# Pooled attention with its queries in blocks of 64, 64 and 16 and its keys split into 128 and 16

## The chip, the cores and the metric

The kernel runs on one core of one Trainium2 chip. The metric is the device time of one execution in microseconds (µs). Five engines work side by side, each through its own instructions in order, and wait for each other by semaphores: TensorE (PE in the profile, with PEld for its weight loads), VectorE (DVE), ScalarE (ACT), GpSimd (POOL) and SyncE (SP), which here only issues DMAs. POOL also issues the DMAs that add to what already lies in on-chip memory.

## The reference

Two attentions are added, and the sum goes through a gated layer without nonlinearity. `q`, `k` and `v` are 8 x 8 x 576 x 64 in fp32 (batch, head, position, feature).

```python
factor = 4; Sd = S // factor                       # 144 pooled positions
q_d = q.reshape(B, H, Sd, factor, D).mean(axis=3)  # and k_d, v_d
out_d = sm_attn(q_d, k_d, v_d)                     # softmax over 144 keys
out_up = np.repeat(out_d, factor, axis=2)
mask = np.abs(pos[:, None] - pos[None, :]) < factor
out_local = softmax(where(mask, scale * q @ k.T, -1e9)) @ v
x = (out_up + out_local)  ->  (4608, 512)
a = x @ w1;  b = x @ w2
out = (a * b @ w3) @ w_out
```

Only the pooled attention, `out_d`, is touched by the change.

## The kernel before

**The order of the work.** The kernel first lists all its work as tasks (`Plan.add`): an engine, an estimated cost, the tasks it depends on, and the rings of buffers it takes. `Plan.order` then plays the list through many times, backward and forward, with different allowances, and keeps the order that a replay with random delays finds best. The program is written out in that order, and within an engine the order is fixed. So a change of one task's cost can rearrange work anywhere. A ring of `n` buffers lets a task start when the task `n` before it has let go.

**The stages.** The program folds `w3 @ w_out` on PE (`accw`, line 351), splits weights into two fp32r parts, and works through 24 units (8 batches, 3 each). A unit computes the local attention and adds the pooled one; two units make a chunk of 384 tokens for the gated layer (`moe`): 24 matmuls of 384 columns into each pair of `pab` tiles (lines 269 to 271), and 9 matmuls of 512 columns into `acc` for each of eight slices. The two `pab` banks are freed by ACT (`a<-pab`, line 912) and DVE (line 914). The units of batches 0 and 1 do the local attention on PE in groups (`se_ps`, `te_ps`, `oe_ps`), those of batches 2 to 7 on DVE and ACT (`pr`, `pv`, `xl`), with some sums as accumulating DMAs on POOL (`xl<-pv`, line 842).

**The pooled attention** (`pooled` and `quad`, lines 418 to 535) is done once per batch:
- The four positions of a pool are summed. For batches 2 to 7 `qks` and `vs` are loaded once by SP and three times added to by POOL's accumulating DMAs (lines 433 and 434). For batches 0 and 1 only `vs` is. `vs` holds the 144 keys as two halves of 72 on 72 partitions, a row of 4 KB for each.
- Heads are handled in two quads of two pairs of heads. The scores (`s_ps`, line 482) of a quad are 12 matmuls over 64 features in 64x64 tiles of PE: three blocks of queries (from 0, 48 and 80; 64 in each, so that they overlap), two pairs, two parities of the head. Each gives 144 columns.
- DVE takes the maximum (`gmx`, line 487), ACT the exponential with its sum (`pexp`, line 496; six instructions), DVE the reciprocal, and POOL (line 511), for batches 0 and 1 ACT (line 508), scales.
- PE transposes `pexp` (`t_ps`, line 521; 12 transposes per quad, to 72 partitions), and ACT copies the result into `pt` (line 528, three copies).
- PE multiplies `pt` with `vs` (`o_ps`, line 449; 32 matmuls over 72 keys in 72x32 tiles, two halves for each result), and ACT copies into `oup` (lines 457 and 459).

`pexp`, `pt`, `vs` and `qks` have one buffer each, and `s_ps`, `t_ps` and `o_ps` share three PSUM banks with the group attention.

Of the kernel before, what the change touches and what calls it, by code (L numbers as in the profile page):

```python
# [9 lines left out]
F32 = mybir.dt.float32  # L10
# [11 lines left out]
FAC = 4  # L22
SD = S // FAC
SB = SD // 16
NB = 16
# [7 lines left out]
NT = 3  # L33
THIRDS = [(0, 0), (48, 0), (80, 16)]
# [28 lines left out]
AHEAD = 4  # L63

# [15 lines left out]
class Task:  # L80
    __slots__ = ("eng", "cost", "fn", "deps", "late", "rings", "after")

    def __init__(self, eng, cost, fn, deps, late, rings, after):
        self.eng, self.cost, self.fn, self.deps, self.late, self.rings, self.after = eng, cost, fn, deps, late, rings, after


class Plan:

    def __init__(self):
        self.tasks = []  # L90

    def add(self, eng, cost, fn, deps=(), take=(), uses=(), late=0.0):
# [7 lines left out]
        t = Task(eng, cost, fn, [d for d in deps if d is not None], late, rings, after)  # L100
# [91 lines left out]

    def order(self):
# [19 lines left out]
        return [self.tasks[i] for i in self.best[3]]  # L213
# [26 lines left out]
def tile_attention_moe(ctx: ExitStack, tc: tile.TileContext, q, kw, vw, qk4, v4, w1, w2, w3, wout, edge, out):  # L240
# [15 lines left out]
    nc.scalar.activation(out=junk, in_=junk, func=AF.Exp)  # L256

# [63 lines left out]

    def out_weight(j):
# [7 lines left out]
    def fold():  # L330
# [3 lines left out]

        def block(m, hf):
            T, _, tx, h = words(w3[m, hf].unsqueeze(1), lambda: pools["early"].tile([128, 512], F32, name="w3", bufs=BUFS["w3"]), [R["w3"]], "early")
            xs[m, hf] = T, tx, h

        def product(m, j):
# [22 lines left out]

        def part(m, hf):
# [24 lines left out]
    def gate_weights(g):  # L388
# [6 lines left out]
        for wi, wsrc in enumerate((w1, w2)):  # L395
            for k0 in range(0, KT, parts):
                src = wsrc[min(g, 1), k0:k0 + parts, :, at:at + n].rearrange("k p n -> p k n")
                T, ld, tx, wx = words(src, lambda: pools[pool].tile([128, nw], F32, name="wx", bufs=BUFS[pool + "_wx"]), [R[pool + "_wx"]], pool, parts)
                ld.deps += before

                def high(T=T, wi=wi, k0=k0):
                    if gates[wi][g] is None:
                        both = [wpool, pools.get("wlate")][g - 1].tile([128, 2, KT, 2, n], F32R, name=["wo", "wb"][g - 1])
                        for i in range(2):
                            gates[i][g] = both[:, i]
                    T["p"] = gates[wi][g][:, k0:k0 + parts]
                    nc.scalar.copy(out=T["p"][:, :, 0], in_=T["x"].rearrange("p (k n) -> p k n", k=parts))
                th = add("ACT", act_us(nw), high, [tx] + (folded if g == 1 else []), uses=[wx])
                tl = add("DVE", dve_us(nw), lambda T=T: nc.vector.tensor_tensor(out=T["p"][:, :, 1], in0=T["x"].rearrange("p (k n) -> p k n", k=parts), in1=T["p"][:, :, 0].bitcast(F32), op=ALU.subtract), [th], uses=[wx])
                users += [th, tl]  # L410
                g_ready.setdefault((wi, g), []).extend([th, tl])
# [4 lines left out]

    def pooled(b):
# [6 lines left out]

        def first_v():
            raws[b][1] = work.tile([QB, 2, H, D], F32, name="vs", bufs=BUFS["vs"])
            nc.sync.dma_start(out=raws[b][1], in_=v4[b, 0])
        if b not in PB:
            lq, hq = add("SP", 0.5, first_qk, take=[R["qks"]], late=dma_us(128 * 4608))
        lv, hv = add("SP", 0.5, first_v, [lq], take=[R["vs"]], late=dma_us(QB * 4096))  # L430
        for f in range(1, FAC):
            if b not in PB:
                lq = add("Pool", 1.04, lambda f=f: nc.gpsimd.dma_start(out=raws[b][0], in_=qk4[b, f], accum_op=ALU.add), [lq], uses=[hq], late=dma_us(128 * 4608, True))
            lv = add("Pool", 1.04, lambda f=f: nc.gpsimd.dma_start(out=raws[b][1], in_=v4[b, f], accum_op=ALU.add), [lv], uses=[hv], late=dma_us(QB * 4096, True))
# [8 lines left out]
        def values():  # L443
            for dh in range(2):
                P["o", dh] = ps.tile([128, 2, SD], F32, tag="g", name="o_ps", bufs=BUFS["ps"])
# [631 lines left out]
```

## Time and profile before

| | |
|---|---|
| time, median of 3 runs | 783.5 µs (782.77 to 785.19) |
| the profiled execution's own time | 783.63 µs |
| its span, first to last instruction | 781.9 µs |
| granted TensorE clock, mean | 0.993 |
| busy: PE, DVE, ACT, POOL | 752.5, 613.0, 540.0, 115.8 µs |
| DMA packets | 42548, 111.92 MB |

The profile is one execution, and the difference of 1.7 µs between its time and its span lies ahead of the first instruction and behind the last. A line of the profile names the source line (L482), the engine, the operation, what is written and read by the program's tile names, the shapes and a count. Matmuls overlap, and the end of each is modelled: what a matmul costs is read from one start to the next, not from its duration.

### The profile page before, as it was taken

What the parts mean: (1) busy time and instruction counts of PE and PEld (TensorE: products, weight loads), DVE (VectorE), ACT (ScalarE), POOL (GpSimd) and SP (SyncE); (2) the same over time, 40 slices, a digit from 0 to 9 for tenths busy, and PEclk for the clock granted to TensorE, in tenths of its full rate; (3) what the DMA queues carried; (4) which work ended last, traced back from release to release, by engine and by line L of the source; (5) the groups of instructions that cost most, each with busy time, mean ns of one, the idle gap of its engine ahead of it and who ended that gap; (6) DMA issues with size and microseconds to landing.
All of it is one profiled execution on the core that took longest, in us unless ns stands there. A gap on an engine that the chain in (4) does not pass through costs nothing.

```text
span 781.9 us, 15058 instructions
## 1 busy us (share of the span) xinstructions
PE 752.5 (96%) x5320; PEld 654.8 (84%) x5320; DVE 613.0 (78%) x1049; ACT 540.0 (69%) x2120; POOL 115.8 (15%) x139
## 2 busy tenths in 40 slices
PE   4889999999999999999999999999999999999995
PEld 1445588898999899999999999998999999999994
DVE  4457966749999999989999998998998998963110
ACT  5788898647978688666787686776785787841211
POOL 1000011000221122211121222110221220110000
PEclk9999999999999999999999999999999999999998
DMA  8995779433576727856549739854469544350101
GB/s 291 305 252 182 230 190 218 81 104 103 117 181 177 149 63 202 202 99 171 127 88 224 172 80 216 169 119 135 119 134 224 122 114 120 63 100 1 41 0 41
DMA packets 42548, 111.92 MB, mean 143 GB/s; under 512 B 5080, under 2 KB 11224, under 8 KB 42472
## 3 DMA queue, kind: packets, MB, share of 16 engines
q0 software_dynamic: 12672, 38.94, 28.9%
q1 hardware_dynamic: 29800, 72.01, 28.5%
q8 instruction: 42, 0.69, 0.4%
q14 instruction: 34, 0.28, 0.1%
HBM read 80.26 MB, written 9.44 MB: 115 GB/s over the span
## 4 chain that ended last, share of the span: by engine, by line
PE 73%; issue 7%; DMA 7%; DVE 6%; ACT 5%; POOL 1%; SPq 1%; POOLq 0%; ACTq 0%; DVEq 0%
PE pab L269 14%; PE pab L270 14%; PE pab L271 14%; PE acc L269 7%; PE acc L271 7%; PE acc L270 7%; PE accw L351 3%; DMA raw<-in_w_dram 3%; PE t_ps L521 2%; DMA raw<-in_wout_dram 2%; PE o_ps L449 2%; ACT pexp L496 1%; DVE pr L767 1%; DMA xl<-pv 1%; PE s_ps L482 1%
## 5 line engine op out<-in xcount | busy, mean ns | idle before, releaser
L777 ACT ACTIVATE junk<-pr 128x64 f32<-128x64 f32 x432 | 110.8, 257 | 19.0 <-DVE pr L767 8.4
L767 DVE TENSOR_TENSOR pr<-q_t,kv 128x768 f32<-128x768 f32 x126 | 119.8, 973 | 3.6 <-DMA kv<-in_kw_dram 3.5
L826 ACT ACTIVATE pv<-kv,s_t 128x64 f32<-128x64 f32 x432 | 114.5, 342 | 10.3 <-DVE s_t L803 5.9
L269 PE MATMUL acc<-wphl,gh 128*128 128x512 f32 x288 | 115.5, 401 | 0.0
L271 PE MATMUL acc<-wphl,gl 128*128 128x512 f32 x288 | 113.8, 395 | 0.0
L270 PE MATMUL acc<-wphl,gh 128*128 128x512 f32 x288 | 113.6, 394 | 0.0
L912 ACT COPY a<-pab 128x384 f32<-128x384 f32 x96 | 45.9, 478 | 79.9 <-PE pab L271 66.5
L914 DVE TENSOR_TENSOR a<-pab,a 128x384 f32<-128x384 f32 x96 | 53.2, 554 | 53.5 <-PE pab L271 48.8
L842 POOL DMA_DIRECT2D xl<-pv x54 | 47.2, 875 | 311.4 <-DVE xl L844 249.7
L919 ACT CAST gh<-a 128x384 fp32r<-128x384 f32 x96 | 49.2, 513 | 59.4 <-PE acc L270 52.1
L780 DVE TENSOR_REDUCE s_t<-pr 128x12 f32<-128x768 f32 x90 | 84.1, 944 | 0.1
L777 ACT ACTIVATION_READ_ACCUMULATOR junk<-pr 128x1 f32 x432 | 81.1, 188 | 0.0
L351 PE MATMUL accw<-wo,w 128*128 128x512 f32 x128 | 64.4, 638 | 15.5 <-DVE w L316 12.2
L921 DVE TENSOR_TENSOR gl<-a,gh 128x384 fp32r<-128x384 f32 x96 | 53.9, 562 | 27.9 <-ACT gh L919 27.5
L834 DVE TENSOR_TENSOR pv<-kv,s_t 128x768 f32<-128x768 f32 x72 | 69.8, 979 | 0.1
L269 PE MATMUL pab<-xh,wo 128*128 128x384 f32 x192 | 66.3, 346 | 0.5 <-ACT a L912 0.5
L269 PE MATMUL pab<-xh,w2a 128*128 128x384 f32 x192 | 66.1, 344 | 0.3 <-DVE a L914 0.2
L269 PE MATMUL pab<-xh,w1a 128*128 128x384 f32 x192 | 66.2, 345 | 0.0
L269 PE MATMUL pab<-xh,wb 128*128 128x384 f32 x192 | 65.8, 343 | 0.2
L270 PE MATMUL pab<-xl,w2a 128*128 128x384 f32 x192 | 65.7, 342 | 0.0
L271 PE MATMUL pab<-xh,w2a 128*128 128x384 f32 x192 | 65.5, 341 | 0.0
L271 PEld LDWEIGHTS acc<-wphl,gl 128*128 128x128 f32 x288 | 54.1, 188 | 13.2
(109 smaller groups left out, 1718.6 us busy)
## 6 DMA issues: line engine op xcount, KB each, us to landing
xl<-pv POOLq DMA_DIRECT2D x54, 384.0 KB, 4.3
raw<-in_w_dram SPq DMA_DIRECT2D x32, 512.0 KB
qks<-in_qk_dram POOLq DMA_DIRECT2D x18, 576.0 KB, 7.4
kv<-in_kw_dram SPq DMA_DIRECT2D x18, 576.0 KB
kv<-in_vw_dram SPq DMA_DIRECT2D x18, 576.0 KB
vs<-in_v_dram POOLq DMA_DIRECT2D x24, 288.0 KB, 6.5
q_t<-in_q_dram SPq DMA_DIRECT2D x18, 384.0 KB
out_dram<-o_sb SPq DMA_DIRECT2D x24, 256.0 KB
```

The lines of the kernel that those rows point to most:

```text
L269: nc.tensor.matmul(out_ps, lhsT=lh, rhs=rh, start=first, stop=False)
L270: nc.tensor.matmul(out_ps, lhsT=lh, rhs=rl, start=False, stop=False)
L271: nc.tensor.matmul(out_ps, lhsT=ll, rhs=rh, start=False, stop=last)
L351: nc.tensor.matmul(accs[m], lhsT=T["x"][:, j % 4 * 128:j % 4 * 128 + 128], rhs=wo[0][:, j], start=j == 0, stop=j == NF - 1)
L767: (nc.gpsimd if o in share["qk_pool"] else nc.vector).tensor_tensor(out=T[o], in0=T["q"], in1=T["k"][:, o * D:o * D + nq].rearrange("p (t ...
L777: nc.scalar.activation(out=junk, in_=T[o][:, t], func=AF.Copy, accum_out=T["s"][:, t, o:o + 1])
L780: reds.append(add("DVE", dve_us(nq), lambda o=o: nc.vector.tensor_reduce(out=T["s"][:, :, o], in_=T[o], op=ALU.add, axis=AX.X), [tp], uses ...
L826: nc.scalar.mul(out=T["pv", o][:, tt], in_=T["v"][:, (tt + o) * D:(tt + o + 1) * D], mul=T["s"][:, tt, o:o + 1])
L834: nc.vector.tensor_tensor(out=T["pv", o], in0=T["v"][:, o * D:o * D + nq].rearrange("p (t d) -> p t d", d=D), in1=T["s"][:, :, o].unsqueez ...
L914: tg = add("DVE", dve_us(CT), lambda f=f: nc.vector.tensor_tensor(out=T["a", f], in0=T["p", 1, f], in1=T["a", f], op=ALU.mult), [ta, ends[ ...
L919: nc.scalar.copy(out=T["gh", f], in_=T["a", f])
L921: tl = add("DVE", dve_us(CT), lambda f=f: nc.vector.tensor_tensor(out=T["gl", f], in0=T["a", f], in1=T["gh", f].bitcast(F32), op=ALU.subtr ...
```

## The change

The 144 queries of all heads are now cut into 64, 64 and 16. The first quad has two blocks (queries 0 to 63 and 64 to 127 of its two pairs), the second these two and a third that holds the last 16 queries of all four pairs (it computes the last 32 and uses 16), in 64x32 tiles. The keys are split into 128 and 16: each score matmul becomes a wide one (128 columns) and a narrow one (16), and both parities lie side by side in a tile `pexp`, now allocated once for the whole kernel, with 16 columns of zeros between them, so that the 16 last keys of both heads are transposed together. A block has three transposes of 128x128 instead of four of 112 or 128 by 72.

`v` is loaded as `vs` (128 keys on 128 partitions) and `vl` (16 keys), each with its own DMAs in rows of 2 KB, and `vl` is copied once within on-chip memory to partitions 32 to 47, by ACT (by DVE for batches 0 and 1), for the other parity. The values become 16 matmuls over 128 keys and 16 over 16 keys in 32x32 tiles, the latter at row 0 for one parity and at row 32 for the other. `o_ps` is now one tile per parity instead of one per half of the features.

The planner gains names for groups of tasks and a list of shifts (`SHIFTS`), which is empty; after the search it now plays the best priorities through once more (`self.final`), with an allowance of 0.1 and transfers 1.1 times as long, and that order is written out.

```diff
-NT = 3
-THIRDS = [(0, 0), (48, 0), (80, 16)]
+QM = 64
+QR = SD - 2 * QM
+KM = 64
+KR = SD - 2 * KM
+PW = 128 + KR
...
-        return [self.tasks[i] for i in self.best[3]]
+        prio = list(self.best[1])
...
+        self.final = self.run(prio, 0.1, slow=1.1)
+        return [self.tasks[i] for i in self.final[3]]
...
+    soft = wpool.tile([128, 3, 2 * PW + 16], F32, name="pexp")
+    nc.vector.memset(soft[:, :, PW:PW + 16], 0.0)
...
+        def load_v(f, add=False):
+            dma = (lambda **kw: nc.gpsimd.dma_start(accum_op=ALU.add, **kw)) if add else nc.sync.dma_start
+            return [lambda: dma(out=raws[b][1], in_=v4[b, f, :KM].rearrange("p k h d -> k p (h d)")),
+                    lambda: dma(out=raws[b][2][:KR], in_=v4[b, f, KM:].rearrange("p k h d -> k p (h d)"))]
...
-            lv = add("Pool", 1.04, lambda f=f: nc.gpsimd.dma_start(out=raws[b][1], in_=v4[b, f], accum_op=ALU.add), [lv], uses=[hv], late=dma_us(QB * 4096, True))
+            lv = [add("Pool", 1.04, ld, [t], uses=[hv], late=dma_us(n * 2048, True)) for ld, t, n in zip(load_v(f, True), lv, (128, KR))]
+        if b in PB:
+            lv.append(add("DVE", dve_us(H * D, True), lambda: nc.vector.tensor_copy(out=raws[b][2][32:], in_=raws[b][2][:KR]), lv[1:], uses=[hv]))
+        else:
+            lv.append(add("ACT", act_us(H * D), lambda: nc.scalar.copy(out=raws[b][2][32:], in_=raws[b][2][:KR]), lv[1:], uses=[hv]))
...
-                    for kb in range(2):
-                        for Q in range(NQ):
-                            nc.tensor.matmul(P["o", dh][32 * Q:32 * Q + 32, par], lhsT=raws[b][1][:, kb, 2 * Q + par, dh * 32:dh * 32 + 32], rhs=P["pt"][:, Q, par, kb], start=kb == 0, stop=kb == 1)
+                    for Q in range(NQ):
+                        h = (2 * Q + par) * D + dh * 32
+                        nc.tensor.matmul(P["o", par][32 * Q:32 * Q + 32, dh], lhsT=raws[b][1][:, h:h + 32], rhs=P["pt"][:, Q, par], start=True, stop=False)
+                for par in range(2):
+                    r = 32 * par
+                    for Q in range(NQ):
+                        h = (2 * Q + par) * D + dh * 32
+                        nc.tensor.matmul(P["o", par][32 * Q:32 * Q + 32, dh], lhsT=raws[b][2][r:r + KR, h:h + 32], rhs=P["pt"][r:r + KR, Q, 2], start=False, stop=True)
...
+        nt = 2 + qd
...
-            for i, (q0, _) in enumerate(THIRDS):
-                for w in range(2):
+            for i in range(nt):
+                m, ws, q0 = (32, range(NQ), SD - 32) if i == 2 else (QM, (2 * qd, 2 * qd + 1), QM * i)
+                for w, pair in enumerate(ws):
                     for par in range(2):
-                        qk = raws[b][0][par * D:par * D + D, :, 2 * qd + w]
-                        nc.tensor.matmul(T["s"][par][w * GQ:w * GQ + GQ, i], lhsT=qk[:, 0, q0:q0 + GQ], rhs=qk[:, 1], start=True, stop=True)
+                        qk = raws[b][0][par * D:par * D + D, :, pair]
+                        ks = qk[:, 1].rearrange("p (k s) -> p k s", k=2)
+                        for of, at in ((ks[:, :, :KM], KR * par), (ks[:, :, KM:], 128 * (1 - par))):
+                            nc.tensor.matmul(T["s"][par][w * m:w * m + m, i, at:at + of.shape[1] * of.shape[2]], lhsT=qk[:, 0, q0:q0 + m], rhs=of, start=True, stop=True)
...
-                for par in range(2):
-                    for kb in range(2):
-                        nc.tensor.transpose(out=T["t"][i][:, par, kb, :n], in_=T["p"][:n, par, i, kb * QB:kb * QB + QB], identity=ident[:n, :n])
+                for x, at in enumerate((0, PW + 16 + KR, 128)):
+                    nc.tensor.transpose(out=T["t"][i][:, x], in_=T["p"][:, i, at:at + 128], identity=ident)
```

On PE, at the first scores of batch 2 (`s_ps` from `qks`, between matmuls of the gated layer), there stood before

```order
L269 MATMUL pab<-xh_1649,w2a 128x384
L270 MATMUL pab<-xl_1650,w2a 128x384
L271 MATMUL pab<-xh_1649,w2a 128x384
L482 MATMUL s_ps<-qks 64x144 x12
L269 MATMUL acc_1209<-wphl,gh 128x512
```

and there stands now

```order
L301 MATMUL pab<-xh_1681,w1a 128x384
L302 MATMUL pab<-xl_1682,w1a 128x384
L303 MATMUL pab<-xh_1681,w1a 128x384
L547 MATMUL s_ps<-qks 64x128
L547 MATMUL s_ps<-qks 64x16
```

where the last two rows follow each other eight times in all, sixteen times in the second quad. A wide and a narrow matmul of the same tile stand next to each other.

On PE, at the values of batch 2 (`o_ps`, ahead of the third group of gate weights before and of the first now), there stood before

```order
L269 MATMUL pab<-xh_2049,w2a 128x384
L270 MATMUL pab<-xl_2050,w2a 128x384
L271 MATMUL pab<-xh_2049,w2a 128x384
L449 MATMUL o_ps<-pt,vs 32x144 x32
L269 MATMUL pab<-xh_2049,wo 128x384
```

and there stands now

```order
L301 MATMUL pab<-xh_2083,w2a 128x384
L302 MATMUL pab<-xl_2084,w2a 128x384
L303 MATMUL pab<-xh_2083,w2a 128x384
L504 MATMUL o_ps<-pt,vs 32x144 x8
L509 MATMUL o_ps<-pt,vl 32x144 x8
L504 MATMUL o_ps<-pt,vs 32x144 x8
L509 MATMUL o_ps<-pt,vl 32x144 x8
```

The block keeps its number of matmuls, in four runs that change between tiles of 128x32 and 32x32.

On POOL, at the accumulations of v of batch 5 (`qks` is the load of queries and keys, `xl` a sum of the local attention), there stood before

```order
L433 DMA qks<-in_qk_dram 128x1152
L434 DMA vs<-in_v_dram 72x1024
L842 DMA xl<-pv 128x768
L434 DMA vs<-in_v_dram 72x1024 x2
L842 DMA xl<-pv 128x768
```

and there stands now

```order
L482 DMA qks<-in_qk_dram 128x1152
L467 DMA vl<-in_v_dram 16x1x512
L467 DMA vs<-in_v_dram 128x1x512
L915 DMA xl<-pv 128x768
L467 DMA vl<-in_v_dram 16x1x512
L467 DMA vs<-in_v_dram 128x1x512
L467 DMA vl<-in_v_dram 16x1x512
L467 DMA vs<-in_v_dram 128x1x512
```

Six issues stand where three stood, and the third of `vl` comes behind the second of `vs`.

More of the change, by code (lines that the diff above doesn't have):

```diff
@@ L90, in __init__, with named, run @@
         self.tasks = []
+        self.group = ""
+    def named(self, fn):
+        def run(*a):
+            old, self.group = self.group, " ".join([fn.__name__] + [str(x) for x in a if isinstance(x, int)])
+            r = fn(*a)
+            self.group = old
+            return r
+        return run
     def add(self, eng, cost, fn, deps=(), take=(), uses=(), late=0.0):
@@ L99, in add @@
             after += last[:1]
-        t = Task(eng, cost, fn, [d for d in deps if d is not None], late, rings, after)
+        t = Task(eng, cost, fn, [d for d in deps if d is not None], late, rings, after, self.group)
         for h in list(got) + list(uses):
@@ L191, in replay, with again @@
         return max(end)
+    def again(self, prio):
+        now = self.run(prio, 0.1)
+        back = self.run([-x for x in now[2]], 0.05, back=True, slow=1.1)
+        return [-x for x in back[2]]
     def order(self):
@@ L394, in gate_weights @@
         parts = 512 // n
-        for wi, wsrc in enumerate((w1, w2)):
-            for k0 in range(0, KT, parts):
[L397 to L411, printed above, removed]
@@ L827, in unit @@
                     if t0 == 0:
[L828 removed]
+                        tm, h = add("ACT", TOKENS * act_us(D, 1), mult, [norm, lv], take=[ring], uses=[hv, hs])
                     else:
```

123 lines of the change are left out of this document (84 added, 39 removed).

## The prediction

> **What bounds the kernel now.** I read the page's first part, then the windows by stage, then who waits for whom on the matrix engine (PE), then its timeline.
>
> ```profile
> PE 752.5 (96%) x5320; PEld 654.8 (84%) x5320; DVE 613.0 (78%) x1049; ACT 540.0 (69%) x2120; POOL 115.8 (15%) x139
> ```
>
> The busy share says PE, but a pipelined matmul can look busy while it waits. The windows (busy time of each engine, granted clock, DMA share, GB/s) and the waits of PE from 160 µs on settle it:
>
> ```profile
> 20.00:60.00 40.00, 35.76 (x202) 17.23 (x200) 21.04 (x47) 30.14 (x74) 2.65 (x3) 1.00 0.95 281
> 60.00:100.00 40.00, 37.43 (x455) 20.16 (x449) 33.49 (x87) 35.68 (x106) 0.00 (x0) 1.00 0.61 193
> 100.00:160.00 60.00, 58.90 (x783) 52.26 (x784) 40.65 (x101) 49.37 (x178) 7.74 (x9) 0.97 0.68 157
> ...
> 180.00:680.00 500.00, 499.04 (x3205) 458.27 (x3204) 466.38 (x715) 382.63 (x1671) 98.28 (x104) 1.00 0.61 142
> 680.00:782.00 102.00, 92.56 (x481) 85.73 (x480) 31.34 (x51) 25.70 (x63) 3.42 (x4) 0.96 0.17 39
> ```
> ```profile
> PE pab L269 <- ACT a L912: 0.5, 1, 0.5
> PE pab L269 <- DVE a L914: 0.2, 1, 0.2
> ```
>
> From 160 µs to the end PE waits 0.7 µs. The pace of its matmuls says the same (start, duration, instruction): 0.17 µs from one gate matmul to the next at 300 µs, where VectorE (DVE) is 93% busy (466.38 of 500), and again at 725 µs, where little runs beside PE.
>
> ```profile
> 300.29 0.34 PE L270 MATMUL pab<-xl,w1a 128*128 128x384 f32 x1
> 300.46 0.34 PE L271 MATMUL pab<-xh,w1a 128*128 128x384 f32 x1
> 300.73 0.97 PE L482 MATMUL s_ps<-qks 64*64 64x144 f32 x24
> 301.62 0.44 PE L269 MATMUL pab<-xh,w2a 128*128 128x384 f32 x1
> ```
> ```profile
> 724.98 0.34 PE L271 MATMUL pab<-xh,w1a 128*128 128x384 f32 x1
> 725.15 0.34 PE L269 MATMUL pab<-xh,w2a 128*128 128x384 f32 x1
> ```
>
> So PE time removed after 160 µs is taken off the end. The tile view of the values' result (copies per batch two: first and last start) says which batches lie there: 2 to 7, while 0 and 1 are done by 125 µs, where PE waits for weights:
>
> ```profile
> L459 ACT COPY oup<-o_ps x12: 377/390/402, 248.1 to 655.3; 128x288 f32<-128x288 f32 x12
> L457 ACT COPY oup<-o_ps x4: 398/400/418, 59.2 to 125.3; 128x288 f32<-128x288 f32 x4
> ```
> ```profile
> PE accw L351 <- DVE w L316: 12.2, 4, 8.3
> ```
>
> I count nothing for them.
>
> **The change on PE.** What a block costs is the distance from its first start to the next block's. Two blocks in 64x64 tiles (scores with 144 and group scores with 72 columns) and two in 72x32 tiles (values with 144 and group values with 64) give the price of a column:
>
> ```profile
> 149.22 0.64 PE L655 MATMUL se_ps<-k,qn 64*64 64x72 f32 x24
> 149.79 0.44 PE L269 MATMUL pab<-xh,wb 128*128 128x384 f32 x1
> ```
> ```profile
> 316.69 2.17 PE L449 MATMUL o_ps<-pt,vs 72*32 72x144 f32 x64
> 318.79 0.44 PE L269 MATMUL pab<-xh,wb 128*128 128x384 f32 x1
> ```
> ```profile
> 165.58 1.56 PE L697 MATMUL oe_ps<-pte,v_w 72*32 72x64 f32 x96
> 167.06 0.50 PE L269 MATMUL acc<-wphl,gh 128*128 128x512 f32 x1
> ```
>
> An fp32 matmul is two passes (x24 for 12 matmuls), and four tiles fit the array, so I count rounds of four passes. Scores: 6 rounds of 144, 864 columns, 0.89 µs; group scores: 432 columns, 0.57; so 0.74 ns a column and 0.25 fixed. Values: 16 rounds of 144, 2304 columns, 2.10; group values: 24 rounds of 64, 1536 columns, 1.48; so 0.81 ns and 0.24 fixed. Entering a tiled block costs 0.09 besides (0.27 from 300.46 to 300.73, less 0.18). Per batch before: scores 2 x 0.98 = 1.96, values 2.19.
>
> The transposes run untiled:
>
> ```profile
> 48.08 1.37 PE L521 MATMUL t_ps<-ident,pexp 112*72 112x112 f32 x12
> 49.28 1.02 PE L351 MATMUL accw<-wo,w 128*128 128x512 f32 x2
> ```
> ```profile
> 68.41 0.82 PE L626 MATMUL te_ps<-ident,se 128*72 128x128 f32 x6
> 69.06 0.60 PE L351 MATMUL accw<-wo,w 128*128 128x512 f32 x1
> ```
>
> Twelve cost 1.20, so 2.40 per batch; one with 128 columns costs 0.65/6 = 0.108.
>
> After the change:
> - **Scores.** The first quad has two blocks, each of four wide (128 keys) and four narrow (16 keys) matmuls: 576 columns and four narrow rounds. The second has a third block of eight tiles of 64x32; if eight run at once it adds 288 columns. By columns alone: 0.09 + 0.25 + 0.43 = 0.77 and 0.09 + 0.25 + 0.64 = 0.98. A narrow round costs between its 0.012 by columns and the 0.052 of a 64-column round (64 x 0.81); I add 0.02 to each of the ten, halfway, as no row is nearer. The change of tiling ahead of the third block costs between nothing and 0.34 (a fixed part and an entry); I take the entry's 0.09, the only row of such a change by itself. So 0.85 + 1.19 = 2.04: **+0.08**. Eight tiles at once is not in the trace; in both modes it shows, as many run as fit, so I take eight. Four would add 0.21.
> - **Transposes.** 6 + 9 full ones: 15 x 0.108 = 1.62, **-0.78**. Weights of 128 columns instead of 72 are loaded for each; if that set the pace, the 0.175 of a gate matmul, which loads as many, is the upper bound: 2.63, +0.23.
> - **Values.** 16 matmuls over 128 keys (8 rounds) and 16 over 16 keys in 32x32 tiles (4 rounds if eight run at once): 1728 columns, 0.09 + 0.24 + 1.40 = 1.73. They alternate, three changes of tiling inside; at 0.09 each 2.00: **-0.19**. Bounds: 1.73 with free changes; 0.47 more with four at once and 1.02 for changes at 0.34, 3.22.
>
> Per batch 2.04 + 1.62 + 2.00 = 5.66 for 6.55: **-0.89**, and -5.3 µs for six. The profiled execution took 783.63 (span 781.9 and 1.7 around it), 0.13 over the median of 783.5. **Forecast 778.3 µs.** At the lower bounds (narrow and tiling free) the batch saves 0.21 + 0.78 + 0.46 = 1.45; for all eight 11.6, 772. At the upper ones scores cost 0.93 + (0.98 + 0.24 + 0.34 + 0.21) = 2.70, and the batch loses 0.74 + 0.23 + 1.03 = 2.0: 799.6. All upper ends together need four misreadings of one sign.
>
> The narrow matmuls are where a page speaks against the change: the Trainium skill, "TensorEngine Tiling", section "Instruction Overhead", gives each matmul about 60 cycles, so that a narrow one costs as much as one with 60 columns. As an estimate by that page a narrow round is 60 x 0.74 = 0.044 instead of 0.032, 0.12 more per batch, and the sum would give 779.0; no row here has fewer than 64 columns.
>
> **The other engines.** Grouped by shape (count, busy, mean ns):
>
> ```profile
> L496 ACT ACTIVATE pexp<-s_ps,gnb 128x144 f32<-128x144 f32 x96 | 35.4, 386 | 2.4 <-DVE gnb L488 2.0
> L511 POOL TENSOR_TENSOR pexp<-pexp,grs 128x432 f32<-128x432 f32 x24 | 29.6, 1261 | 93.5 <-ACT pv L826 51.7 <-DVE grs L504 29.6 <-ACT junk L777 11.6
> L434 POOL DMA_DIRECT2D vs<-in_v_dram x24 | 22.9, 956 | 139.0 <-DMA vs<-in_v_dram 138.0 <-PE pab L271 0.9
> L929 ACT COPY o_sb<-acc 128x512 f32<-128x512 f32 x36 | 20.5, 580 | 8.5 <-DMA out_dram<-o_sb 6.8 <-PE acc L271 1.6
> L496 ACT ACTIVATION_READ_ACCUMULATOR pexp<-s_ps,gnb 128x1 f32 x96 | 20.2, 211 | 0.0
> L528 ACT COPY pt<-t_ps 72x384 f32<-72x384 f32 x48 | 20.0, 474 | 0.0
> L487 DVE TENSOR_REDUCE gmx<-s_ps 128x3 f32<-128x432 f32 x32 | 18.0, 599 | 1.9 <-PE s_ps L482 1.8
> ```
>
> ScalarE (ACT) loses two exponentials per batch (2 x 0.60) and one and a half copies (0.7), and gains the copy of vl (0.58, as the 512 wide o_sb): -1.3. DVE loses a third of two maxima (0.4), POOL a third of two products (0.8), and gains three issues (2.9). All of it lies beside PE (383, 466 and 98 of 500 busy), so it counts nothing. Without that cover ACT's -1.3 and DVE's -0.4 would still be gains. The bytes of v are the same, in twice as many rows of half the length; from 180 µs the DMA engines are 61% busy.
>
> **A wait is added:** ACT now waits for the last accumulation into vl, where before only PE waited for v. Behind it on ACT stand the copies `a<-pab` that free PE's two gate banks. It is tightest in batch 5, whose three issues and first exponential were:
>
> ```profile
> 430.86 0.89 POOL L434 DMA_DIRECT2D vs<-in_v_dram  x1
> ...
> 437.80 1.21 POOL L434 DMA_DIRECT2D vs<-in_v_dram  x1
> 444.46 0.83 POOL L434 DMA_DIRECT2D vs<-in_v_dram  x1 [5.45 <-DMA vs<-in_v_dram]
> ```
> ```profile
> 452.42 0.39 ACT L496 ACTIVATE pexp<-s_ps,gnb 128x144 f32<-128x144 f32 x1
> ```
> ```profile
> DMA to landing us min/median/max: 4.4/6.5/11.3
> ```
>
> The third vl issue stands behind the second of vs, so near 439; it lands near 445, and ACT comes to the copy just ahead of the exponentials, near 449. I cost it at nothing, with 4 µs to spare.
>
> **The rivals.**
> 1. *The gain is given back* (0.17): with PE faster, DVE ends the wait. For it: 93% busy from 180 to 680. Against it: PE waits 0.7 µs now. Then only DVE's six times 0.4 is left, 2.4: 781.2, or a little more with new waits: 782.
> 2. *The tiles stop overlapping in the scores* (0.11, slower): a narrow matmul stands between two wide ones of the same tile, four passes in a row. If PE starts the next tile only when the last of these has begun, a matmul pair costs 2 x 0.095 + 0.012 = 0.20 (128 columns at 0.74 ns); 8 and 16 pairs give 1.6 + 0.34 and 3.2 + 0.43, 5.6 for 1.96. The batch loses 3.6 - 0.97 = 2.7, six 16: 799. It decides from scores of 2.9 on (the gain gone), about two tiles at once. Against it: two passes of one tile stand in a row today, and 24 passes of 0.107 still take 0.89, four abreast. The Trainium skill, "TensorE: Matmul & The Clock Gate", Part 3, states the rule that would do it, "MATMULs are pc-monotone in start AND end — strict FIFO, no reordering"; by that rule today's 24 passes would take nearly twice their 0.89, so this trace does not agree.
> 3. *ACT waits for vl* (0.07): a landing of 11.3 instead of 6.5 is 4.8 late; less the 2.1 µs of one gate bank (12 x 0.175) 2.7 for each of two batches eats the gain: 783.7.
> 4. *The new order starts worse* (0.05, slower): instructions of the first 100 µs are rearranged, where loads take 95% of the DMA time; a few µs, 788.
> 5. *Narrow rounds and changes of tiling are nearly free* (0.10): 772 to 776.
>
> **How the numbers follow.** The forecast (776 to 781.2) has 0.50. With about 0.3% (2.35 µs) as what a measurement can tell from none: faster 0.50 + 0.10 = 0.60, same 0.17 + 0.07 = 0.24, slower 0.16. The range takes in rivals 1 and 3 and most of 5: 773 to 786.5.
>
> **What would show it.** PE's starts: first scores 0.76, second 1.10 without entry, six transposes 0.65, nine 0.97, values 1.91; PE's waits after 160 µs still under 2 µs. Wrong if scores take 1.5 and more (rival 2), if PE waits for `a` or DVE (1), if ACT idles ahead of `vl` (3), or if the first gate matmul starts later than before (4).

## The result, and the profile after

The changed kernel takes **1023.93 µs** (median of 4 runs, 1023.04 to 1028.5), the kernel before 784.35 on the same chip (782.77 to 785.62): a ratio of **1.308**, with a 95% interval of 1.305 to 1.311. The forecast of 778.3 and its range of 773 to 786.5 are both far off, and so is the sign. Below, a run's time is the median of all its executions, and ratios compare the fast ones alone: three runs have one slow execution each (2570, 1902 and 794.6 µs) that is in no ratio.

The page of the profiled execution (its own time 1024.09, its span 1022.3): busy times, DMA packets and the queue of the accumulating DMAs (packets, MB, share of 16 engines), the chain that ended last, and two groups of DMA issues with their median time to landing.

```profile
PE 796.1 (78%) x5632; PEld 684.2 (67%) x5632; DVE 603.0 (59%) x1052; ACT 529.7 (52%) x2082; POOL 146.7 (14%) x163
...
DMA packets 69174, 112.14 MB, mean 110 GB/s; under 512 B 29400, under 2 KB 35544, under 8 KB 69096
...
q0 software_dynamic: 38784, 39.13, 23.7%
...
DMA 44%; PE 40%; issue 8%; DVE 3%; POOL 2%; ACT 2%; SPq 1%; POOLq 0%; DVEq 0%; ACTq 0%
DMA vs<-in_v_dram 17%; DMA vl<-in_v_dram 13%; DMA xl<-pv 9%; PE pab L301 8%; PE pab L302 8%; PE pab L303 8%; PE acc L303 4%; PE acc L301 4%; PE acc L302 4%; DMA raw<-in_w_dram 1%; PE accw L386 1%; PE o_ps L504 1%; PE s_ps L547 1%; DMA k<-in_qk_dram 1%; DMA qks<-in_qk_dram 1%
...
xl<-pv POOLq DMA_DIRECT2D x54, 384.0 KB, 6.1
...
vs<-in_v_dram POOLq DMA_DIRECT2D x24, 256.0 KB, 15.0
```

PE is no longer what sets the end: the chain holds 44% of DMA, and three transfers stand at its head. An accumulation into `vs` lands in 15.0 µs where it took 6.5, with a ninth fewer bytes in it (256 KB for 288; the others are in `vl`). The queue moves the same 39 MB as in the kernel before, in three times the packets. The same rows on the page of before:

```profile
q0 software_dynamic: 12672, 38.94, 28.9%
...
xl<-pv POOLq DMA_DIRECT2D x54, 384.0 KB, 4.3
...
vs<-in_v_dram POOLq DMA_DIRECT2D x24, 288.0 KB, 6.5
```

Who waited for whom (µs in total, times, longest), the whole span:

```profile
POOL vs L467 <- DMA vs<-in_v_dram: 179.8, 15, 15.7
POOL vl L467 <- DMA vl<-in_v_dram: 152.8, 17, 68.4
...
PE pab L301 <- ACT a L987: 112.4, 15, 18.8
...
ACT vl L488 <- DMA vl<-in_v_dram: 67.8, 4, 25.7
...
DVE xl L917 <- DMA xl<-pv: 65.9, 8, 15.0
```

POOL's instructions around 350 µs (start, duration, and in brackets how long it stood idle before and for what) show how one late landing spreads:

```profile
349.37 0.92 POOL L467 DMA_DIRECT2D vl<-in_v_dram  x1 [10.77 <-DMA vl<-in_v_dram]
350.12 1.54 POOL L467 DMA_DIRECT2D vs<-in_v_dram  x1
350.93 1.67 POOL L915 DMA_DIRECT2D xl<-pv  x1
353.28 0.91 POOL L467 DMA_DIRECT2D vl<-in_v_dram  x1 [0.69 <-DMA vl<-in_v_dram]
364.69 1.35 POOL L467 DMA_DIRECT2D vs<-in_v_dram  x1 [10.50 <-DMA vs<-in_v_dram]
366.49 0.89 POOL L467 DMA_DIRECT2D vl<-in_v_dram  x1 [0.45 <-DMA vl<-in_v_dram]
367.28 1.02 POOL L915 DMA_DIRECT2D xl<-pv  x1
383.74 1.37 POOL L467 DMA_DIRECT2D vs<-in_v_dram  x1 [15.43 <-DMA vs<-in_v_dram]
384.57 2.62 POOL L577 TENSOR_TENSOR pexp<-pexp,grs 128x288 f32<-128x288 f32 x2
```

Each accumulation into `vs` waits for the one before it, and POOL runs its instructions in order, so two of them hold up POOL from 350 to 384. Behind them stand the sums `xl<-pv` of the local attention and the scaling of `pexp`. DVE, which needs `xl`, waits 65.9 µs, ACT waits 67.8 for `vl`, and the copies `a<-pab` that free PE's gate banks stand behind these on both engines: PE loses 112.4 µs to ACT. The first gate matmul starts at 133.4 µs, where it started at 96.1.

Two windows of the same execution (busy time of PE, PEld, DVE, ACT and POOL, granted clock, DMA share, GB/s). In the second an accumulation into `vs` is the only large transfer under way:

```profile
180.00:680.00 500.00, 403.96 (x3073) 362.54 (x3074) 335.65 (x558) 278.22 (x1201) 86.81 (x88) 0.89 0.48 109
...
358.50:362.50 4.00, 3.66 (x19) 2.93 (x17) 0.00 (x0) 1.12 (x7) 0.00 (x0) 1.00 0.15 28
```

There the DMA engines are 15% busy, 2.4 of 16, and move 28 GB/s. Over the long window the granted clock is 0.89, where it was 1.00, so a part of PE's longer busy time (796.1 for 752.5) is the same work at a lower clock: the first kernel of the next section has the same instructions on PE, but for the order of the keys, and is busy for 750.2 µs, at a clock of 0.990.

### The profile page after: what moved, and what is told of

Its sections match the earlier page's. It is cut to its first block, busy times and chain, and to the rows that moved or that the text cites. A ratio compares the mean times of both kernels' runs of the same rounds, so it can differ in the third digit from the quotient of the medians.

```text
span 1022.3 us, 15690 instructions
## 1 busy us (share of the span) xinstructions
PE 796.1 (78%) x5632; PEld 684.2 (67%) x5632; DVE 603.0 (59%) x1052; ACT 529.7 (52%) x2082; POOL 146.7 (14%) x163
## 3 DMA queue, kind: packets, MB, share of 16 engines
q0 software_dynamic: 38784, 39.13, 23.7%
## 4 chain that ended last, share of the span: by engine, by line
DMA 44%; PE 40%; issue 8%; DVE 3%; POOL 2%; ACT 2%; SPq 1%; POOLq 0%; DVEq 0%; ACTq 0%
DMA vs<-in_v_dram 17%; DMA vl<-in_v_dram 13%; DMA xl<-pv 9%; PE pab L301 8%; PE pab L302 8%; PE pab L303 8%; PE acc L303 4%; PE acc L301 4%; PE acc L302 4%; DMA raw<-in_w_dram 1%; PE accw L386 1%; PE o_ps L504 1%; PE s_ps L547 1%; DMA k<-in_qk_dram 1%; DMA qks<-in_qk_dram 1%
## 5 line engine op out<-in xcount | busy, mean ns | idle before, releaser
L899 ACT ACTIVATE pv<-kv,s_t 128x64 f32<-128x64 f32 x432 | 116.9, 340 | 57.2 <-DMA xl<-pv 40.6
L301 PE MATMUL pab<-xh,w1a 128*128 128x384 f32 x192 | 73.5, 383 | 78.8 <-ACT a L987 77.6
L989 DVE TENSOR_TENSOR a<-pab,a 128x384 f32<-128x384 f32 x96 | 53.1, 553 | 112.4 <-PE pab L303 56.9
L301 PEld LDWEIGHTS pab<-xh,w1a 128*128 128x128 f32 x192 | 40.6, 212 | 85.6 <-ACT a L987 81.8
L917 DVE TENSOR_TENSOR xl<-xl,pv 128x768 f32<-128x768 f32 x54 | 51.4, 953 | 77.5 <-DMA xl<-pv 65.9
L915 POOL DMA_DIRECT2D xl<-pv x54 | 54.2, 1004 | 285.5 <-DVE xl L917 228.3
L301 PE MATMUL pab<-xh,wo 128*128 128x384 f32 x192 | 69.2, 361 | 26.1 <-DVE a L989 17.2
L386 PE MATMUL accw<-wo,w 128*128 128x512 f32 x128 | 68.2, 675 | 16.6 <-DVE w L348 16.6
L301 PE MATMUL pab<-xh,w2a 128*128 128x384 f32 x192 | 68.8, 358 | 13.3 <-DVE a L989 13.3
```

The costliest lines, as they stand in the source:

```text
L301: nc.tensor.matmul(out_ps, lhsT=lh, rhs=rh, start=first, stop=False)
L386: nc.tensor.matmul(accs[m], lhsT=T["x"][:, j % 4 * 128:j % 4 * 128 + 128], rhs=wo[0][:, j], start=j == 0, stop=j == NF - 1)
L899: nc.scalar.mul(out=T["pv", o][:, tt], in_=T["v"][:, (tt + o) * D:(tt + o + 1) * D], mul=T["s"][:, tt, o:o + 1])
L915: t = add("Pool", 1.04, lambda o=o: nc.gpsimd.dma_start(out=T["x"], in_=T["pv", o], accum_op=ALU.add), [t, tm], uses=[hx, h], late=dma_us( ...
L989: tg = add("DVE", dve_us(CT), lambda f=f: nc.vector.tensor_tensor(out=T["a", f], in0=T["p", 1, f], in1=T["a", f], op=ALU.mult), [ta, ends[ ...
```

## The experiments

Theory 1: the source pattern of the new transfers is at fault. `v4[b, f, :KM].rearrange("p k h d -> k p (h d)")` reads first the even and then the odd rows, so its outermost dimension is 2, and the rows go to few DMA engines. Theory 2: rows of 2 KB are slow by themselves. Theory 3: the new order of the plan, or ACT's new wait. Theory 4: the small transfers of 16 partitions (`vl`). Theories 5 and 6 came up on the way and are about the rest, the gain on PE that does not come out: other engines give it back (5), or the order of the tasks eats it (6).

**Rows in memory order.** Only the order of the rows of `v` (and of the keys in the scores) is changed:

```diff
-v4[b, f, :KM].rearrange("p k h d -> k p (h d)")   # the same for KM:
+v4[b, f, :KM].rearrange("p k h d -> (p k) (h d)")
-ks = qk[:, 1].rearrange("p (k s) -> p k s", k=2)
+ks = qk[:, 1].rearrange("p (k s) -> p s k", k=2)
...
```

> The changed kernel with one thing undone: the rows of v are read in the order in which they lie in memory (one run of 128 rows and one of 16), instead of first all the even and then all the odd ones, and the scores take the keys in that same order. Rows are still 2 KB, PE, DVE and ACT have the same instructions in the same order, POOL as many issues. Theory 1 (a source pattern whose outermost size is 2 gives the rows to few DMA engines): vs lands in about 6.5 us as before instead of 15.0, PE's waits after 160 us fall under 5 us, and the sum of the prediction comes back: 777 to 782. Theory 2 (rows of 2 KB are slow by themselves): vs still lands in 10 us or more, over 850. Theory 3 (the new order of the plan or the new wait of ACT for vl): about 1000, as in the changed kernel. Theory 4 (the copies and accumulations of 16 partitions): about 1000.

Measured: 783.39 µs (12 runs), ratio 1.000 to the kernel before (0.998 to 1.002). On its page:

```profile
q0 software_dynamic: 14592, 38.94, 29.1%
...
xl<-pv POOLq DMA_DIRECT2D x54, 384.0 KB, 4.5
...
vs<-in_v_dram POOLq DMA_DIRECT2D x24, 256.0 KB, 5.5
```

`vs` lands in 5.5 µs with rows of 2 KB, the same order of the tasks and the same added wait of ACT for `vl`: theories 2, 3 and 4 are out as causes of the 240 µs. It is 1.4 µs above theory 1's interval; that rest is taken up below.

**The pattern alone, in the kernel before.** Its rows of 4 KB are dealt out by patterns of outermost size 2, 4 and 8:

```diff
-in_=v4[b, f]
+in_=v4[b, f].rearrange("(p g) k h d -> g p k h d", g=2)   # 4, 8
-rhs=qk[:, 1]
+rhs=qk[:, 1].rearrange("p (k s g) -> p k g s", k=2, g=2)
```

> The kernel before with one thing of the change done alone: v's 72 rows of 4 KB are read first the even and then the odd ones (a source pattern of outermost size 2), and the scores take the keys in that order. Rows, bytes, issues, order of all engines as before. Theory 1: about 36 rows of 0.4 us on each of a few engines, so vs lands in 13 to 18 us instead of 6.5, what is queued behind it is late as well, and the time is 850 to 1050. Theory 2 (rows of 2 KB): 784, since the rows are still 4 KB. Theories 3 and 4: 784.

> The kernel before with v's rows of 4 KB dealt out by a pattern of outermost size 4 (every fourth row first). With outermost size 2 vs landed in 14.9 us, before in 6.5. Theory 1 (as many engines as the outermost size): 18 rows on each of 4 engines instead of 36 on each of 2; on a line through 36 rows at 14.9 and 6 rows (12 engines divide 72 rows) at 6.1 to 6.5 that is 9.6 to 9.9 us, and the time lies between, 795 to 880. Rival (rows apart from each other are slow whatever the size): 14 to 16 us and about 1000.

> The same with outermost size 8. Theory 1: 9 rows on each of 8 engines, vs lands in 7.0 to 7.3 us and the time is 784 to 795. Rival (rows apart are slow whatever the size): 14 to 16 us and about 1000.

Measured: 998.15, 850.73 and 804.99 µs, ratios of 1.274 (1.269 to 1.279), 1.085 (1.081 to 1.088) and 1.028 (1.024 to 1.031). The queue's packets and the landing of `vs` on the three pages, size 2, then 4, then 8:

```profile
q0 software_dynamic: 24576, 39.03, 23.0%
...
vs<-in_v_dram POOLq DMA_DIRECT2D x24, 288.0 KB, 14.9
```
```profile
q0 software_dynamic: 17664, 38.98, 26.8%
...
vs<-in_v_dram POOLq DMA_DIRECT2D x24, 288.0 KB, 9.7
```
```profile
q0 software_dynamic: 14208, 38.95, 27.9%
...
vs<-in_v_dram POOLq DMA_DIRECT2D x24, 288.0 KB, 7.3
```

The pattern alone, on the old kernel with its old rows, makes nine tenths of the loss. The three landings lie in their intervals, and so do the times of sizes 2 and 4. If a transfer runs on as many engines as its outermost size, 36, 18 and 9 rows fall to each; the landings 14.9, 9.7 and 7.3 lie on a line of 0.27 to 0.29 µs per row.

The trace does not name the engine of a packet, but it records each packet's start, duration and size, and these count how many rows are under way at once. While rows of an accumulation into `vs` are under way, it is two of them for 78% of the time at size 2, four for 60% at size 4, and eight, the most frequent number, for 37% at size 8; in the kernel before, 14 and 15 are the most frequent. One row of 4 KB takes 0.33 µs in all four traces (median), and one row of 2 KB 0.18 in the changed kernel as with rows in memory order. So no row became slower: fewer of them go at once. That is theory 1, and the 15% above, 2.4 of 16, agrees with it.

The Trainium skill, "DMA: Bandwidth & Descriptors", section "Why a DMA increments its semaphore by 16 and not by 1", has the rule: a transfer runs on the largest number of engines up to 16 that divides the slowest dimension larger than 1 on both sides. By it the patterns of these runs run on 2, 4 and 8 engines, and the changed kernel's on 2; the counts agree. For the 72 rows of the kernel before it gives 12, as an expectation above has it, and there the records do not agree with it: for 42% of the time more than 12 rows are under way, where at size 8 more than 8 are for 17%. The section names an exception on trn2 for some copies issued by GpSimd, 16 engines with the rows per engine rounded up, here five; that would use 15.

The times of sizes 4 and 8 hold something else too: a score block there takes 1.69 µs instead of 0.90, which is told at the end. For the 12 blocks of batches 2 to 7 that is 9.5 µs. Without it the three sizes cost 214, 58 and 12 µs, and 24 times the extra landing is 202, 77 and 19: at size 2 all of it comes out at the end, at size 4 three quarters, at size 8 less. Size 8 lay above its interval of 784 to 795 by about the price of its scores.

**Only `vl` apart.** The first kernel of this section, with the changed kernel's order for the last 16 keys alone:

```diff
-v4[b, f, KM:].rearrange("p k h d -> (p k) (h d)")
+v4[b, f, KM:].rearrange("p k h d -> k p (h d)")
```

> The kernel of the first run of this set (128 rows of v in memory order), but the last 16 rows, vl, read even ones first as in the changed kernel. Theory 1: 8 rows of 0.2 us on each engine are short, vl lands in 4 to 6 us, and the time is within 1% of that kernel, 777 to 790. Theory 4 (vl is the culprit): near 1000. Theory 3: about 1000.

Measured: 785.25 µs, ratio 1.0016 (1.0002 to 1.003). At most 0.3%, 2.4 µs: theory 4 is out as a main cause. `vl` lands in 5.1 µs there, inside its interval.

**Two transfers instead of one.** The changed kernel's order of keys, each transfer cut by `k`:

```diff
+for k in range(2):
+    dma(out=raws[b][i][k * n:k * n + n], in_=v4[b, f, p0:p0 + n, k].rearrange("p h d -> p (h d)"))
```

> The changed kernel with its even-then-odd order of keys, but each transfer of v is cut into two, one for the even rows and one for the odd ones, so that each has one run of 64 (or 8) rows of 2 KB that lie 4 KB apart. The same bytes go to the same places, order of all engines as in the changed kernel, twice as many issues on POOL (48 more of about 0.9 us). Theory 1: 64 and 8 rows are dealt out widely again, vs lands in 5 to 7 us, 783 to 795 with the issues. Theory 2 (rows of 2 KB that lie apart are slow): vs lands in 10 us and more, over 850.

Measured: 783.84 µs, ratio 1.0003 (0.999 to 1.0016). `vs` lands in 4.7 µs, a little under its interval, though its rows of 2 KB lie 4 KB apart, and 48 more issues on POOL cost nothing that shows. So the rows' distance is no cause either: what matters in these runs is that the outermost dimension is long.

**The new order alone.** The kernel before with the change's last replay of the plan:

```diff
-return [self.tasks[i] for i in self.best[3]]
+self.final = self.run(list(self.best[1]), 0.1, slow=1.1)
+return [self.tasks[i] for i in self.final[3]]
```

> The kernel before, with only the planner's last step of the change: the best order's priorities are run once more with slack 0.1 and transfers at 1.1 of their cost, and that order is used. No instruction is added or taken away. Theories 1, 2 and 4: within 0.7% of before, 779 to 789 (rival 4 of the prediction put a worse order at a few us). Theory 3 (the order is at fault): 850 or more.

Measured: 791.19 µs, ratio 1.0107 (1.008 to 1.013). Far too little for theory 3, and 2 µs outside what the other theories gave it: with the old tasks this replay costs 7.5 µs.

**Where the gain on PE went.** Mended, the change is worth nothing, 783.4 for 783.6, where 5.3 µs were forecast. The next kernels lay `v` out key by key, so that the first 128 keys are 128 rows in a row and the scores read runs of 128 and 16 keys:

```diff
-"v4": v.reshape(B, H, 2, QB, FAC, D).transpose(0, 4, 3, 2, 1, 5),
+"v4": v.reshape(B, H, SD, FAC, D).transpose(0, 3, 2, 1, 4),
...
-for of, at in ((ks[:, :, :KM], KR * par), (ks[:, :, KM:], 128 * (1 - par))):
+for of, at in ((qk[:, 1, :128], KR * par), (qk[:, 1, 128:], 128 * (1 - par))):
```

> The changed kernel with the keys in their natural order everywhere: v is laid out key by key (its transposition ahead of the launch is another one), so the first 128 keys are 128 rows in a row and the last 16 are 16 more, and the scores read runs of 128 and 16 keys. Order of all engines as in the kernel with v's rows in memory order. That kernel's score blocks took 0.92 and 1.47 us because keys 288 bytes apart are read; the changed kernel's, with runs of 64 and 8, took 0.82 and 1.32. If the transfers are all that was wrong (theory 1) and the score price follows the runs: 0.25 less per batch, 1.5 to 2.0 less than 783.4, so 781.4 to 782. Theory 5 (the gain on PE is given back by other engines, rival 1 of the prediction): 783 to 784.

The second differs in the order alone:

```diff
-return [self.tasks[i] for i in self.final[3]]
+return [self.tasks[i] for i in self.best[3]]
```

> The same kernel, but the plan takes the best order that it found, as before, and leaves out the change's last replay with slack 0.1. The kernel before lost 7.5 us by that replay alone. Theory 6 (the replay eats the gain that PE has made): 774 to 778. Theory 5: within 2 us of the kernel with natural keys.

Measured: 783.48 µs (ratio 0.9996, 0.998 to 1.002) and 784.35 (0.9998, 0.997 to 1.003). The first lies in theory 5's interval and not in theory 1's, but these are closer to each other than the interval is wide (±0.2%, 1.6 µs). The second says that on this task list the last replay is not what eats the gain; theory 6's 774 to 778 failed. PE's timeline in the first, around the two score blocks and the values of one batch, gives the prices that the prediction estimated (each ends where the next starts):

```profile
359.26 0.89 PE L546 MATMUL s_ps<-qks 64*64 64x128 f32 x32
360.08 0.50 PE L301 MATMUL acc<-wphl,gh 128*128 128x512 f32 x1
```
```profile
396.45 1.39 PE L546 MATMUL s_ps<-qks 64*64 64x128 f32 x64
397.77 0.44 PE L301 MATMUL pab<-xh,w1a 128*128 128x384 f32 x1
```
```profile
411.59 0.70 PE L504 MATMUL o_ps<-pt,vs 128*32 128x144 f32 x16
412.22 0.47 PE L509 MATMUL o_ps<-pt,vl 16*32 16x144 f32 x16
412.63 0.70 PE L504 MATMUL o_ps<-pt,vs 128*32 128x144 f32 x16
413.25 0.47 PE L509 MATMUL o_ps<-pt,vl 16*32 16x144 f32 x16
413.66 0.50 PE L301 MATMUL acc<-wphl,gh 128*128 128x512 f32 x1
```

Scores 0.82 and 1.32 for twice 0.90, values 2.07 for 2.10. The transposes, in the same place of the program, in the kernel with natural keys and then in the kernel before:

```profile
393.96 0.82 PE L585 MATMUL t_ps<-ident,pexp 128*128 128x128 f32 x6
394.54 0.42 PE L301 MATMUL pab<-xh,w2a 128*128 128x384 f32 x1
...
408.40 1.15 PE L585 MATMUL t_ps<-ident,pexp 128*128 128x128 f32 x9
409.30 0.42 PE L301 MATMUL pab<-xh,wo 128*128 128x384 f32 x1
```
```profile
296.30 1.37 PE L521 MATMUL t_ps<-ident,pexp 112*72 112x112 f32 x12
297.43 0.42 PE L269 MATMUL pab<-xh,w1a 128*128 128x384 f32 x1
```

0.58 and 0.90 for twice 1.13. In all 5.68 per batch for 6.14 (without entries): 0.46 less, not 0.89, and 2.8 µs for six batches. PE's waits in this kernel from 160 µs on:

```profile
PE acc L303 <- DVE gl L995: 3.1, 3, 2.0
PE pab L301 <- DVE a L988: 1.2, 2, 0.6
PE pab L301 <- ACT a L986: 1.0, 1, 1.0
PE t_ps L585 <- POOL pexp L576: 0.8, 2, 0.6
```

6.1 µs for the 0.7 of before, 4.3 of it for DVE: the gain may be there and be given back. To test that, half of the width of DVE's additions is left out, in both kernels, so that their output is incomplete:

```diff
-nc.vector.tensor_tensor(out=T["x"], in0=T["x"], in1=T["pv", o], op=ALU.add)
+nc.vector.tensor_tensor(out=T["x"][:, :UT // 2], in0=T["x"][:, :UT // 2], in1=T["pv", o][:, :UT // 2], op=ALU.add)
```

> The kernel before, but DVE's additions xl<-xl,pv take only half of their width (the other half is left out, so part of the window attention is missing from the output): about 26 us less of DVE's work (54 times 0.48), all orders as before. PE waits only 0.7 us after 160 us in the kernel before, so it should stay at 782 to 784 if PE alone sets its end; 780 or less if DVE sets it too. It is the base for the next run.

> The changed kernel with natural keys, and the same half of DVE's additions left out. Its blocks on PE take 5.68 us per batch where those of the kernel before take 6.14, so 0.46 less, 2.8 for six batches, and yet both took 783.5. Theory 5 (PE's gain is there, and DVE being late gives it back): relieved of 26 us DVE work it is 2.5 to 4 us faster than the kernel before with the same relief, and PE's waits fall from 6 us to under 2. Theory 6 (the order of the tasks, or loads of the first 100 us, eat the gain): within 1.2 us of that kernel, with PE's waits after 160 us still 4 and more or its first 160 us later.

Measured: 783.15 (ratio 0.9993, 0.998 to 1.0006) and 781.09 (0.9965, 0.995 to 0.998). The additions fell from 52.7 to 30.3 µs in the kernel before, so the relief was 22 µs and not 26. Relieved of it the kernel before stays where it was. The changed one is 2.1 µs faster than that on the same chip, a little under theory 5's 2.5 to 4, and outside theory 6's 1.2. Against itself without relief it gains 2.4, with intervals that just overlap. So most of PE's gain of 2.8 comes out once DVE has less to do, which points at DVE as a cause that holds it back. But PE's waits fell only to 5.0 µs. That is what theory 6 gave, not theory 5's 2, so DVE is not shown to be the whole of it (that profiled execution, of 782.76, is the longest of the twelve, and a typical one may wait less).

**Without narrow scores.** For batches 2 to 7 the odd heads' keys lie turned by 16 places, so one matmul of 144 columns does the work of 128 and 16:

```diff
+turned[len(PB):, :, D:] = np.roll(turned[len(PB):, :, D:], KR, axis=-1)
-for of, at in ((qk[:, 1, :128], KR * par), (qk[:, 1, 128:], 128 * (1 - par))):
+for of, at in ((qk[:, 1], 0),) if b not in PB else (...):
```

> The kernel with natural keys, where for batches 2 to 7 the odd heads' keys lie turned by 16 places (last 16 first, by another transposition ahead of the launch), so the scores need no narrow matmuls: one of 144 columns instead of 128 and 16. By before's 0.90 for six rounds of 144 columns (0.74 ns a column and 0.25 fixed) the first block should take 0.68 instead of 0.82, the second 0.98 instead of 1.32, 0.48 less per batch and 2.9 for six. Theory 5: half or more of that is given back again by waits, 781 to 783.5. If PE alone set the end: 780 to 781.

Measured: **780.7 µs**, ratio 0.9977 (0.9957 to 0.9997), the only version with the whole output that is faster than the kernel before, by about 1.8 µs (0.2 to 3.4). The median lies in the interval for PE alone, 781.5 by the ratio in theory 5's: this run does not tell the two apart. Its two score blocks, in two pieces of PE's timeline:

```profile
363.17 0.72 PE L546 MATMUL s_ps<-qks 64*64 64x144 f32 x16
363.82 0.50 PE L301 MATMUL acc<-wphl,gh 128*128 128x512 f32 x1
```
```profile
400.18 1.13 PE L546 MATMUL s_ps<-qks 64*64 64x144 f32 x32
401.24 0.44 PE L301 MATMUL pab<-xh,w1a 128*128 128x384 f32 x1
```

0.65 and 1.06: 0.17 and 0.26 less than with 4 and 6 narrow rounds, 0.043 for each. With the 16 columns that the wide round now has on top (0.012) a narrow round cost 0.055. Against the kernel with natural keys the time fell by 2.8 µs by the medians and 1.5 by the ratios (their intervals overlap), for 2.6 on PE in six batches.

Two more runs were to tell what holds the rest:

> The kernel with natural keys and no narrow scores, with half of DVE's additions xl<-xl,pv left out (part of the window attention is missing from the output), 26 us less of DVE's work. Its score blocks take 0.43 us less per batch than those of the kernel with natural keys (0.651 and 1.057 for 0.822 and 1.318), 2.6 for six. With the relief that kernel took 781.09 us. If PE's time sets the end there: 778.2 to 779. If what is left is set by the order of the tasks (theory 6): 780 to 781.5.

> The kernel with natural keys and no narrow scores (780.7 us), with the plan's best order instead of the change's last replay. Theory 6 (the replay eats gain): 776 to 779. Otherwise 780 to 782, as the two orders of the kernel with natural keys took 783.5 and 784.4.

Measured: 779.78 (ratio 0.9956, 0.994 to 0.997) and 782.77 (1.0004, 0.998 to 1.003). The first lies between its two intervals: with DVE relieved, the 2.6 µs on PE bring 1.3 by the medians and 0.7 by the ratios, and their intervals overlap. The second lies 0.8 above even the other interval: the old rule for the order is no better than the new one, so theory 6 in this form found no support on these tasks. **Open:** in the best version PE's blocks are 0.89 µs per batch shorter than in the kernel before, 5.3 for six (the number of the forecast, by coincidence: other terms make it up), and 1.8 come out. In its profiled execution, of 784.77 and again the longest of twelve, PE waits 6.0 µs after 160 µs instead of 0.7, which is as much as its blocks save. DVE takes a part back, as the relieved pair suggests; what takes the rest is not settled. ACT is a rival that no run relieves: in the kernel with natural keys DVE's `gl` in turn waits 10.3 µs for ACT's `gh`, 7.1 before.

## Why the prediction was wrong

**The bound now, right.** In the kernel before, PE sets the end: with 22 µs of DVE's work taken out it stays at 783.15. What was drawn from it, that PE time removed after 160 µs is taken off the end, holds only in part: with `v` mended, 2.8 µs less on PE brought nothing that could be measured, and 5.3 brought 1.8 (0.2 to 3.4).

**The step that failed: the transfers of `v` were costed at nothing.** The prediction put it as "The bytes of v are the same, in twice as many rows of half the length", and looked only at how busy the DMA engines are in the mean. The rows' length was harmless (5.5 and 4.7 µs with rows of 2 KB). The order in which the source is read was not: with two rows at once under way most of the time, 15.0 µs instead of 6.5, and with the order mended 783.4 instead of 1023.9. The diff shows it in one expression, `k p (h d)` with `k` of 2. A mean share of 61% says nothing on how many engines one transfer gets.

**The added wait, right in its place, wrong in its size.** Rival 3 had ACT waiting for `vl` with gate copies queued behind it, at 783.7 and a chance of 0.07. The wait is in the trace: ACT stands 67.8 µs for `vl`, and PE's longest waits are for ACT. But its landing was bounded by 11.3 µs, the longest of the old transfers, and it was counted for two batches. `vl` landed in 12.8 µs in the median and up to 17.6, and each accumulation waits for the one before it, so the third is late three times over. POOL's queue also holds `xl<-pv`, which the prediction did not name as waiting. With the rows in memory order ACT waits 2.5 µs for `vl` in all: had the landings stayed, a price of nothing would have been close.

**PE's terms.** Transposes -0.78 forecast, -0.78 measured; weights of 128 columns cost nothing. Scores +0.08 forecast, **+0.35** measured; values -0.19 forecast, **-0.03** measured. Two prices were too low. A narrow round was taken at 0.032 and cost 0.055: ten of them make 0.23. The page that spoke against the change, "TensorEngine Tiling" of the Trainium skill, section "Instruction Overhead", gave 0.044 by the estimate in the prediction, nearer to what was measured than the value taken. A change of tiling was taken at 0.09, PE's entry. Without narrow matmuls the third score block takes 1.06 - 0.65 = 0.41, with 0.21 for its two rounds of 144 columns, so the change is near 0.2. In the values the parts take 0.63 and 0.41, of which columns are 0.47 and 0.23: 0.16 to 0.18 each time. Eight tiles at once was right: in the trace's records the first eight passes of that third block, and of the values' second part, start within 0.05 µs. So the sum on PE was -0.46 per batch, half of what was forecast.

**The rivals.** Tiles that stop overlapping (2): did not happen, 0.82 is far from 1.6. In the records of that block the wide passes of four tiles start within 0.04 µs, though in the program each is followed by the narrow one of its own tile. Gain given back (1): happened in the mended kernels: PE's waits rose by 5.4 µs, and with relief at DVE the change was worth 2.1 µs. A worse start or order (4): the first gate matmul was 37 µs later in the changed kernel, but at 95.8 µs with the rows in memory order (96.1 before), so that was the transfers; the new replay cost the old tasks 7.5 µs; on the new ones it made no difference that could be measured. What was missing is a rival in which a transfer of the same bytes becomes slower, and with it the test that the diff allowed: does the new pattern still have a long outermost dimension?

## What to carry to other kernels

When a DMA's access pattern is rearranged, read its outermost dimension before its bytes: with 2 there, 2.4 of 16 engines were busy here and each of 24 accumulations took 9.5 µs longer; cutting it into two transfers, or another order of rows, gave all of it back. A slow transfer on an in-order queue is paid by everything behind it: where it was slowest, its price here was its extra landing times the number of such transfers (240 µs for 228, 214 for 202), and less where it was less slow. And when PE is busy for all of the time with DVE at 93% right behind, only part of what is saved on PE may come out: here 1.8 of 5.3 µs.

## What was not expected of the hardware

**Spread keys slow the scores.** With every fourth or eighth key first (steps of 16 and 32 bytes in the moving operand) a score block of the old kernel takes 1.69 to 1.70 µs instead of 0.90; with every second (8 bytes) 0.93. In the timeline of the kernel with outermost size 4:

```profile
294.10 1.76 PE L482 MATMUL s_ps<-qks 64*64 64x144 f32 x24
295.80 0.50 PE L269 MATMUL acc<-wphl,gh 128*128 128x512 f32 x1
```

The Trainium skill, "SBUF — State Buffer", section "Specifications (TRN2)", gives lines of 16 bytes that need two hits or more for full bandwidth. Steps of 8 bytes keep two, steps of 16 one, and these runs agree. They do not tell all: in the kernel with `v`'s rows in memory order the keys are read in turn from two places 288 bytes apart, and yet its score blocks take only 0.92 and 1.47 µs for 0.82 and 1.32.

**More packets for the same bytes.** At outermost sizes of 2, 4 and 8 the queue has about 7, 3 and 1 packets more for each row than in the kernel before. In the trace's records they are packets of 8 bytes that take 8 to 9 ns each: 504, 216 and 72 for each transfer of 72 rows, and 8 in the kernel before. That is 16 times the rows on one engine (36, 18, 9 and, as above, 5) less the 72, as if each of 16 engines were given the same number of packets; what they are for the trace does not say. They are short, but a jump in the queue's packets is the sign of this loss on the page of a profile: 38784 for 39 MB here, 14592 with the rows in memory order.
